# An attention of channels and a gated layer: the gate's bias through ScalarE, and transposes of v on 32-bit words

## The chip, the cores and the metric

One NeuronCore of a Trainium2 chip runs the whole program. Its engines work side by side, each through its own queue in order: TensorE (PE; its weight loads are shown as PEld), VectorE (DVE), ScalarE (ACT), GpSimd (POOL, which here issues the loads) and SyncE (SP, which issues the stores). They hand work over by semaphores. Matmul results go to PSUM, a small memory that VectorE and ScalarE read and write too; everything else is in SBUF. The metric is the device time of one execution in microseconds.

## The reference

For each of 4 batches, q, k and v are 6336 rows of 256 channels. The attention is over channels, not rows: one 256 x 256 matrix for a batch.

```python
qn = q / (norm of q over the rows + 1e-6);  kn likewise
s  = kn.T @ qn / tau                    # 256 x 256, per batch
a  = softmax(s, axis=-1)
x  = v @ a                              # 6336 x 256
H  = relu(x @ w_h);  T = sigmoid(x @ w_t + b_t)
out = T * H + (1 - T) * x
```

q, k and v are 78 MB of float32 and the output 26 MB.

## The kernel before

**Tiling.** The rows of a batch are cut into 50 slices: 48 of 128 rows and two of 96. In a load, each partition takes rows that lie next to each other, eight slices to a tile (`CH = 8`), and the DMA casts to fp16. Two slices are a *pair*; there are 25 pairs to a batch and 100 in all, numbered g = 25 b + i.

**Stage 1** (`stage1`, L354 to L356) goes over the slices of q and k and accumulates three products in the PSUM tile `sg`: k.T q, and the diagonal blocks of k.T k and q.T q, whose diagonals are the squared norms. For each half c of the channels, a slice takes three matmuls, of 256, 128 and 128 columns, each with a weight load of its own.

**The chain** (`plan_chain`) then makes the softmax on 256 x 256 (L391 to L557), transposes it, multiplies it by the two weight matrices (L590) and leaves `mr`, 256 x 768 in fp16: the columns of a, of a @ w_h and of a @ w_t. It uses VectorE, ScalarE and TensorE in turn. Its broadcast (L512) is the one matmul on fp32 numbers.

**Stage 2** runs over pairs. `transposes` (L628) turns the pair's v, four blocks of 128 x 128 fp16, into the PSUM tile `vt`; `evac_vt` (L634) copies it to SBUF on ScalarE as `vtsb`; `main_xh` (L641) multiplies it by the first 512 columns of mr, for x and x @ w_h, into `xh`. `main_t` multiplies it by the last 256 columns for the gate, into the PSUM tile `t`. A matmul with 512 columns opens t (L653): its weights `row0` are ones in one row and zero elsewhere, its columns `btb` hold the bias in that row, so that every row of t starts as the bias; the four matmuls of L656 add to it. ScalarE then makes relu into `hh` (L676) and the gate as a tanh into `uu` (L684); VectorE makes hh - x (L693), and, for two pairs at a time, the product with the gate (L703) and the result (L722), which SyncE stores.

**Order.** `Plan` is a planner that runs before the kernel is emitted. Each task has an engine, a key, a pitch and a latency in us, the tasks it depends on and the rings of buffers that it takes and gives back (`take`, `drop`). The planner plays the tasks through in time; on TensorE, ScalarE and VectorE it starts, of the tasks that are ready, the one with the lowest key, and the order that it finds becomes each engine's instruction order. Loads go out in the order of their keys. `ENDS` says at which pair stage 1 of batches 1, 2 and 3 is to end: its slices and the loads of q and k are spread evenly over the pairs before (`slot_of`). So stage 1 of the next batch runs between the pairs of the batch before it. The PSUM rings have one buffer each for `sg`, `vt` and `t`, and two for `xh`.

Of the kernel before, what the change touches and what calls it, by code (L numbers as in the profile page):

```python
# [10 lines left out]
f32 = mybir.dt.float32  # L11
f16 = mybir.dt.float16
i32 = mybir.dt.int32

P = 128
# [1 line left out]
QK_BUFS = 9  # L17
V_BUFS = 7
HEAD = 8
ENDS = [16, 41, 68]  # L20


class Ring:
# [136 lines left out]
def kernel(  # L160
# [11 lines left out]
    nc = tc.nc  # L172
    B, N, C = q.shape
# [5 lines left out]
    S = N // P // CH * CH  # L179
# [4 lines left out]
    NP = NS // 2  # L184
    assert NP % 2 == 1

    const = ctx.enter_context(tc.tile_pool(name="consts", bufs=1))
# [7 lines left out]
    plan = Plan()  # L195
# [11 lines left out]
    def new(tag, shape, dt, name):  # L207
        return pool_of.get(tag, work).tile(shape, dt, tag=tag, bufs=nbuf[tag], name=name)


    ident0 = const.tile([P, P], f32, tag="ident0")
    ident = const.tile([P, P], f16, tag="ident")
    ones = const.tile([P, P], f32, tag="ones")
    row0 = const.tile([P, P], f16, tag="row0")
    btb = const.tile([P, 2, C], f16, tag="btb")
    wht = const.tile([P, 2, 2 * C], f16, tag="wht")

    def constants():
# [39 lines left out]
    def sub(nm, b, s):  # L258

        if s < S:  # L260
            return tiles[(nm, b, s // CH)][:, s % CH, :]
        return tiles[(nm, b, NJ)][0:TR, s - S, :]

    def rows(s):
        return P if s < S else TR
# [32 lines left out]
    consts = plan.add("POOL", len(plan.tasks), 0.6, 1.5, [], constants)  # L298
# [45 lines left out]

    def stage1(b, s):

        if s == 0:
            sg_t[b] = new("sg", [P, 2, 512], f32, f"sg{b}")
        sg = sg_t[b]
        qa, ka = sub("q", b, s), sub("k", b, s)  # L350
        first, last = s == 0, s == NS - 1
        for c in range(2):
            cs = bass.ts(c, P)
            nc.tensor.matmul(sg[:, c, 0:C], ka[:, cs], qa, start=first, stop=False)  # L354
            nc.tensor.matmul(sg[:, c, C : C + P], ka[:, cs], ka[:, cs], start=False, stop=False)  # L355
            nc.tensor.matmul(  # L356
                sg[:, c, C + P : C + 2 * P], qa[:, cs], qa[:, cs], start=False, stop=last
            )
# [3 lines left out]
    mr_own = {}  # L362
# [253 lines left out]
    vt_sb = {}  # L616
    vt_ps = {}
    xh_t = {}
    og = {}
    el = {}  # L620

    def transposes(b, i):
        ps = new("vt", [P, 2, 2, P], f16, f"vtps{b}_{i}")
        nr = rows(2 * i)
        for u in range(2):
            src = sub("v", b, 2 * i + u)
            for c in range(2):
                nc.tensor.transpose(ps[:, u, c, 0:nr], src[:, bass.ts(c, P)], ident[0:nr, 0:nr])  # L628
        vt_ps[(b, i)] = ps

    def evac_vt(b, i):
        nr = rows(2 * i)
        vt_sb[(b, i)] = vt = new("vtsb", [P, 2, 2, P], f16, f"vtsb{b}_{i}")
        nc.scalar.copy(out=vt[:, :, :, 0:nr], in_=vt_ps.pop((b, i))[:, :, :, 0:nr])  # L634

    def main_xh(b, i):
        mr, vt, nr = mr_t[b], vt_sb[(b, i)], rows(2 * i)
        xh = new("xh", [P, 2, 2 * C], f32, f"xh{b}_{i}")
        for u in range(2):
            for kt in range(2):  # L640
                nc.tensor.matmul(  # L641
                    xh[0:nr, u, :],
                    vt[:, u, kt, 0:nr],
                    mr[kt][:, 0 : 2 * C],
                    start=(kt == 0),
                    stop=(kt == 1),
                )
        xh_t[(b, i)] = [xh]

    def main_t(b, i):  # L650
        mr, vt, nr = mr_t[b], vt_sb.pop((b, i)), rows(2 * i)
        tt = new("t", [P, 2, C], f32, f"t{b}_{i}")
        nc.tensor.matmul(tt[0:nr, :, :], row0[:, 0:nr], btb, start=True, stop=False)  # L653
        for u in (1, 0):
            for kt in range(2):
                nc.tensor.matmul(  # L656
                    tt[0:nr, u, :],
                    vt[:, u, kt, 0:nr],
                    mr[kt][:, 2 * C : 3 * C],
                    start=False,  # L660
                    stop=(kt == 1 and u == 0),
                )
        xh_t[(b, i)].append(tt)


    def groups_of(b):

        full = NP - 3 if b == B - 1 else NP - 1
        return [[i, i + 1] for i in range(0, full, 2)] + [[i] for i in range(full, NP)]

    def relu(b, i, grp):
        nr, o = rows(2 * i), 2 * (i - grp[0])
        if i == grp[0]:
            for nm in ("hh", "uu", "dd"):
                el[(nm, b, i)] = new(nm, [P, 4, C], f32, f"{nm}{b}_{i}")
        nc.scalar.activation(  # L676
            out=el[("hh", b, grp[0])][0:nr, o : o + 2, :],
            in_=xh_t[(b, i)][0][0:nr, :, C : 2 * C],
            func=Act.Relu,
        )  # L680

    def gate(b, i, grp):
        nr, o = rows(2 * i), 2 * (i - grp[0])
        nc.scalar.activation(  # L684
            out=el[("uu", b, grp[0])][0:nr, o : o + 2, :],
            in_=xh_t[(b, i)][1][0:nr, :, :],
            func=Act.Tanh,
            scale=-0.5,
        )
# [49 lines left out]
            )  # L739


    ready = {}

    def plan_stage1(b):
# [13 lines left out]
    last_o = {}  # L758

    def plan_stage2(b):  # L760
        tr, ev, xh, tt = {}, {}, {}, {}
        for i in range(NP):
            g = b * NP + i
            deps = loaded("v", b, 2 * i) + loaded("v", b, 2 * i + 1) + [consts]
            tr[i] = plan.add(
                "PE", g - 1.6, 0.22, 0.42, deps, lambda i=i: transposes(b, i),
                take=["vt", "vtsb"], drop=drops("v", b, 2 * i + 1),
            )
            ev[i] = plan.add(
                "ACT", g - 1.5, 0.5, 0.64, [tr[i]], lambda i=i: evac_vt(b, i),  # L770
                drop=[(tr[i], "vt")],
            )
            xh[i] = plan.add(
                "PE", g, 0.86, 1.06, [ev[i]] + ready[b], lambda i=i: main_xh(b, i), take=["xh"]
            )
            tt[i] = plan.add(
                "PE", g + 0.1, 0.64, 0.84, [xh[i]] + b_ld, lambda i=i: main_t(b, i),
                take=["t"], drop=[(tr[i], "vtsb")] + ([(mr_own[b], "mr0"), (mr_own[b], "mr1")]
                                                      if i == NP - 1 else []),
            )  # L780
        for grp in groups_of(b):
            us = []
            for i in grp:
                g = b * NP + i
                h = plan.add(
                    "ACT", g, 0.5, 0.63, [xh[i]], lambda i=i, grp=grp: relu(b, i, grp),
                    take=["hh", "uu", "dd"] if i == grp[0] else [],
                )
                h0 = h if i == grp[0] else h0
                us.append(  # L790
                    plan.add(
                        "ACT", g + 0.1, 0.5, 0.63, [tt[i], h],
                        lambda i=i, grp=grp: gate(b, i, grp), drop=[(tt[i], "t")],
                    )
                )
                us.append(
                    plan.add(
                        "DVE", g + 0.2, 0.6, 0.72, [h], lambda i=i, grp=grp: diff(b, i, grp),
                        drop=[(xh[i], "xh")],
                    )  # L800
                )
            d = 0.07 + 0.533 * len(grp)
            m = plan.add(
                "DVE", g + 1.2, d, d + 0.12, us, lambda grp=grp: product(b, grp),
                drop=[(h0, "uu")],
            )
            s = 2 * grp[0]
            j, o, n = s // CH, s % CH, 2 * len(grp)
            tag = "ot" if s >= S else "o"
            r = plan.add(  # L810
                "DVE", g + 1.9, d, d + 0.12, [m], lambda grp=grp: result(b, grp),
                take=[tag] if s >= S or o == 0 else [], drop=[(h0, "hh"), (h0, "dd")],
            )
            if s >= S:
                plan.add(
                    "SP", g + 2, 0.1, 0, [r], lambda: store(b, NJ, 0, 2), drop=[(r, "ot")],
                    size=TR * 2 * C * 4,
                )
                continue
            if o == 0:  # L820
                own = r
            split = b == B - 1 and j == NJ - 1
            if split or o + n == CH:
                lo, cnt = (o, n) if split else (0, CH)
                plan.add(
                    "SP", g + 2, 0.1, 0, [r], lambda j=j, lo=lo, cnt=cnt: store(b, j, lo, cnt),
                    drop=[(own, "o")] if o + n == CH else [], size=P * cnt * C * 4,
                )
# [45 lines left out]
```

## Time and profile before

| | |
|---|---|
| Runs | 307.14, 308.60 and 308.69 us; median 308.6 |
| Profiled execution | 307.13 us, span 305.3 us |
| TensorE busy | 274.8 us (90% of the span), granted clock 0.996 |
| VectorE busy | 204.6 us (67%) |
| ScalarE busy | 178.5 us (58%) |
| HBM | 78.4 MB read, 26.0 MB written |

The span goes from the first to the last instruction of the program; the 1.8 us between it and the execution's time lie around it. Busy time is the union of an engine's instructions. Matmuls are pipelined: the duration of one (222 ns for 128 columns, say) is longer than the step from one to the next, and where the text speaks of the step, it is from the chain of waits, which counts each piece of time once. "x" with a number is a count of instructions.

### The profile page before, as it was taken

What the parts mean: (1) busy time and instruction counts of PE and PEld (TensorE: products, weight loads), DVE (VectorE), ACT (ScalarE), POOL (GpSimd) and SP (SyncE); (2) the same over time, 40 slices, a digit from 0 to 9 for tenths busy, and PEclk for the clock granted to TensorE, in tenths of its full rate; (3) what the DMA queues carried; (4) which work ended last, traced back from release to release, by engine and by line L of the source; (5) the groups of instructions that cost most, each with busy time, mean ns of one, the idle gap of its engine ahead of it and who ended that gap; (6) DMA issues with size and microseconds to landing.
All of it is one profiled execution on the core that took longest, in us unless ns stands there. A gap on an engine that the chain in (4) does not pass through costs nothing.

```text
span 305.3 us, 6171 instructions
## 1 busy us (share of the span) xinstructions
PE 274.8 (90%) x2540; PEld 200.0 (66%) x2540; DVE 204.6 (67%) x321; ACT 178.5 (58%) x336; POOL 48.7 (16%) x96
## 2 busy tenths in 40 slices
PE   0886867999999999999999999999999789999981
PEld 0775855777777777777776777777777445666640
DVE  1000042576677978667677987676767998999995
ACT  1000043565656686666667676666666788998862
POOL 7222442221131221121212121100001000000000
PEclk9999999999999999999999999999999999999998
DMA  6999999999999999999999999999875334333334
GB/s 124 213 215 207 214 208 214 213 233 260 278 244 250 281 216 276 285 226 274 279 247 247 281 232 261 284 250 249 233 207 167 57 137 166 132 143 140 138 138 164
DMA packets 16828, 65.54 MB, mean 215 GB/s; under 512 B 1952, under 2 KB 3616, under 8 KB 13856
## 3 DMA queue, kind: packets, MB, share of 16 engines
q0 software_dynamic: 12608, 39.20, 65.3%
q1 hardware_dynamic: 4192, 25.95, 21.2%
q8 instruction: 20, 0.33, 0.4%
q14 instruction: 8, 0.07, 0.1%
HBM read 78.38 MB, written 25.95 MB: 342 GB/s over the span
## 4 chain that ended last, share of the span: by engine, by line
PE 63%; DVE 18%; DMA 9%; issue 3%; ACT 3%; POOL 1%; ACTq 0%; DVEq 0%; POOLq 0%
PE xh L641 20%; PE sg L354 11%; PE t L656 10%; PE sg L355 6%; PE sg L356 6%; DMA q<-in_q_dram 6%; DVE o L722 6%; DVE dd L693 5%; PE vtps L628 5%; PE t L653 5%; DVE dd L703 5%; DMA k<-in_k_dram 4%; PE ah L590 1%; DVE junk L391 1%; ACT hh L676 1%
## 5 line engine op out<-in xcount | busy, mean ns | idle before, releaser
L354 PE MATMUL sg<-q,k 128*128 128x256 f16 x384 | 93.0, 276 | 14.6 <-DMA k<-in_k_dram 13.9
L641 PE MATMUL xh<-mr,vtsb 128*128 128x512 f16 (+1 forms) x400 | 102.7, 379 | 2.7 <-ACT mr L601 1.6
L693 DVE TENSOR_TENSOR dd<-hh,xh 128x512 f32<-128x512 f32 (+1 forms) x100 | 68.0, 683 | 37.2 <-ACT hh L676 37.1
L676 ACT ACTIVATE hh<-xh 128x512 f32<-128x512 f32 (+1 forms) x100 | 59.6, 597 | 45.8 <-PE xh L641 24.5
L355 PE MATMUL sg<-k 128*128 128x128 f16 x384 | 85.1, 222 | 0.0
L356 PE MATMUL sg<-q 128*128 128x128 f16 x384 | 85.1, 222 | 0.0
L684 ACT ACTIVATE uu<-t 128x512 f32<-128x512 f32 (+1 forms) x100 | 60.4, 604 | 28.7 <-PE t L656 28.5
L703 DVE SCALAR_TENSOR_TENSOR dd<-uu,dd 128x1024 f32<-128x1024 f32 (+2 forms) x53 | 61.6, 1163 | 14.3 <-ACT uu L684 12.9
L656 PE MATMUL t<-mr,vtsb 128*128 128x256 f16 (+1 forms) x400 | 60.0, 273 | 0.0
L722 DVE SCALAR_TENSOR_TENSOR o<-dd,hh 128x1024 f32<-128x1024 f32 (+1 forms) x49 | 58.8, 1200 | 1.0
L634 ACT COPY vtsb<-vtps 128x512 f16<-128x512 f16 (+1 forms) x100 | 57.7, 577 | 2.3 <-PE vtps L628 2.2
L641 PEld LDWEIGHTS <-vtsb 128*128 128x128 f16 (+1 forms) x400 | 36.6, 99 | 29.0 <-issue 4.2
L354 PEld LDWEIGHTS <-k 128*128 128x128 f16 x384 | 38.0, 99 | 21.2 <-DMA k<-in_k_dram 14.6
L656 PEld LDWEIGHTS <-vtsb 128*128 128x128 f16 (+1 forms) x400 | 39.4, 99 | 17.6 <-issue 3.1
L355 PEld LDWEIGHTS <-k 128*128 128x128 f16 x384 | 38.1, 99 | 7.7 <-issue 1.1
L356 PEld LDWEIGHTS <-q 128*128 128x128 f16 x384 | 38.0, 99 | 4.8
L653 PE MATMUL t<-btb,row 128*128 128x512 f16 (+1 forms) x100 | 37.9, 379 | 2.5 <-ACT uu L684 2.5
L628 PE MATMUL vtps<-ident,v 128*128 128x128 f16 x384 | 37.1, 219 | 0.2 <-ACT vtsb L634 0.2
L628 PEld LDWEIGHTS <-v 128*128 128x128 f16 x384 | 29.3, 98 | 9.8 <-issue 0.6
L391 DVE SCALAR_TENSOR_TENSOR junk<-sg,ident 128x128 f32<-128x128 f32 x16 | 4.6, 290 | 35.2 <-PE sg L356 34.8
L254 POOL DMA_DIRECT2D v<-in_v_dram x24 | 12.8, 532 | 80.6 <-PE vtps L628 45.2
L417 ACT ACTIVATE inv<-x 128x4 f32<-128x4 f32 x1 | 0.2, 205 | 38.1 <-DVE junk L391 38.1
(61 smaller groups left out, 116.0 us busy)
## 6 DMA issues: line engine op xcount, KB each, us to landing
out_dram<-o SPq DMA_DIRECT2D x23, 1024.0 KB, 8.8
v<-in_v_dram POOLq DMA_DIRECT2D x24, 512.0 KB, 20.3
q<-in_q_dram POOLq DMA_DIRECT2D x23, 512.0 KB, 20.3
k<-in_k_dram POOLq DMA_DIRECT2D x23, 512.0 KB, 20.5
out_dram<-ot SPq DMA_DIRECT2D x4, 192.0 KB, 6.7
q<-in_q_dram POOLq DMA_DIRECT2D x2, 256.0 KB, 14.6
k<-in_k_dram POOLq DMA_DIRECT2D x2, 256.0 KB, 11.3
out_dram<-o SPq DMA_DIRECT2D x1, 512.0 KB, 2.7
```

The costliest lines, as they stand in the source:

```text
L354: nc.tensor.matmul(sg[:, c, 0:C], ka[:, cs], qa, start=first, stop=False)
L355: nc.tensor.matmul(sg[:, c, C : C + P], ka[:, cs], ka[:, cs], start=False, stop=False)
L356: nc.tensor.matmul(sg[:, c, C + P : C + 2 * P], qa[:, cs], qa[:, cs], start=False, stop=last)
L628: nc.tensor.transpose(ps[:, u, c, 0:nr], src[:, bass.ts(c, P)], ident[0:nr, 0:nr])
L634: nc.scalar.copy(out=vt[:, :, :, 0:nr], in_=vt_ps.pop((b, i))[:, :, :, 0:nr])
L641: nc.tensor.matmul(xh[0:nr, u, :], vt[:, u, kt, 0:nr], mr[kt][:, 0 : 2 * C], start=(kt == 0), stop=(kt == 1),)
L656: nc.tensor.matmul(tt[0:nr, u, :], vt[:, u, kt, 0:nr], mr[kt][:, 2 * C : 3 * C], start=False, stop=(kt == 1 and u == 0),)
L676: nc.scalar.activation(out=el[("hh", b, grp[0])][0:nr, o : o + 2, :], in_=xh_t[(b, i)][0][0:nr, :, C : 2 * C], func=Act.Relu,)
L684: nc.scalar.activation(out=el[("uu", b, grp[0])][0:nr, o : o + 2, :], in_=xh_t[(b, i)][1][0:nr, :, :], func=Act.Tanh, scale=-0.5,)
L693: nc.vector.tensor_tensor(out=el[("dd", b, grp[0])][0:nr, o : o + 2, :], in0=el[("hh", b, grp[0])][0:nr, o : o + 2, :], in1=xh_t[(b, i)][0 ...
L703: nc.vector.scalar_tensor_tensor(out=dd[0:nr, 0:n, :], in0=el[("uu", b, grp[0])][0:nr, 0:n, :], scalar=1.0, in1=dd[0:nr, 0:n, :], op0=AluO ...
L722: nc.vector.scalar_tensor_tensor(out=ot, in0=el[("dd", b, grp[0])][0:nr, 0:n, :], scalar=-0.5, in1=el[("hh", b, grp[0])][0:nr, 0:n, :], op ...
```

## The change

The gate's bias is written into `t` by ScalarE ahead of the gate's matmuls for the pairs g up to `PRESET` = 68. A new constant `bias_all` holds the bias on all partitions in fp32: one matmul at the start spreads it (`spread`), one copy on ScalarE brings it to SBUF (`spread_out`). For each of those pairs a copy on ScalarE (`bias`) takes the buffer of t and fills it, and the gate's four matmuls add to what stands there; L653 falls away. From pair 69 on, L653 is as before.

v is transposed as words of 32 bits, each holding two neighbouring fp16 channels: two transposes of 128 words in place of four of 128 fp16, against the fp32 identity. In `vt` and `vtsb` the even and odd channels of a row then lie alternately, so the weights of `main_xh` and `main_t` are read with a step of two, one half for even and one for odd channels. So that `mr` has its rows in the same order, stage 1 takes k's channels with a step of two as well, as weights (L354, L355) and as columns (L355).

The planner's numbers for these tasks change, `ENDS` goes from 16, 41, 68 to 18, 43, 69, and two edges of dependence are added (the second relu of a group after the first, a result after the one that opened its output tile).

```diff
-ENDS = [16, 41, 68]
+PRESET = 68
+ENDS = [18, 43, 69]
...
+    bias_all = const.tile([P, 2, C], f32, tag="bias_all")
...
         for c in range(2):
             cs = bass.ts(c, P)
-            nc.tensor.matmul(sg[:, c, 0:C], ka[:, cs], qa, start=first, stop=False)
-            nc.tensor.matmul(sg[:, c, C : C + P], ka[:, cs], ka[:, cs], start=False, stop=False)
+            kc = ka.rearrange("p (w two) -> p two w", two=2)[:, c, :]
+            nc.tensor.matmul(sg[:, c, 0:C], kc, qa, start=first, stop=False)
+            nc.tensor.matmul(sg[:, c, C : C + P], kc, kc, start=False, stop=False)
...
     def transposes(b, i):
-        ps = new("vt", [P, 2, 2, P], f16, f"vtps{b}_{i}")
+        ps = new("vt", [P, 2, P], f32, f"vtps{b}_{i}")
         nr = rows(2 * i)
         for u in range(2):
-            src = sub("v", b, 2 * i + u)
-            for c in range(2):
-                nc.tensor.transpose(ps[:, u, c, 0:nr], src[:, bass.ts(c, P)], ident[0:nr, 0:nr])
+            words = sub("v", b, 2 * i + u).bitcast(f32)
+            nc.tensor.transpose(ps[:, u, 0:nr], words, ident0[0:nr, 0:nr])
         vt_ps[(b, i)] = ps
 
     def evac_vt(b, i):
         nr = rows(2 * i)
-        vt_sb[(b, i)] = vt = new("vtsb", [P, 2, 2, P], f16, f"vtsb{b}_{i}")
-        nc.scalar.copy(out=vt[:, :, :, 0:nr], in_=vt_ps.pop((b, i))[:, :, :, 0:nr])
+        vt = new("vtsb", [P, 2, P], f32, f"vtsb{b}_{i}")
+        nc.scalar.copy(out=vt[:, :, 0:nr], in_=vt_ps.pop((b, i))[:, :, 0:nr])
+        vt_sb[(b, i)] = [
+            [vt[:, u, :].bitcast(f16).rearrange("p (n two) -> p two n", two=2)[:, kt, :] for kt in range(2)]
+            for u in range(2)
+        ]
...
-                    vt[:, u, kt, 0:nr],
+                    vt[u][kt][:, 0:nr],
...
+    def preset(b, i):
+        return b * NP + i <= PRESET
+
+    def bias(b, i):
+        nr = rows(2 * i)
+        tt_new[(b, i)] = tt = new("t", [P, 2, C], f32, f"t{b}_{i}")
+        nc.scalar.copy(out=tt[0:nr, :, :], in_=bias_all[0:nr, :, :])
+
     def main_t(b, i):
         mr, vt, nr = mr_t[b], vt_sb.pop((b, i)), rows(2 * i)
-        tt = new("t", [P, 2, C], f32, f"t{b}_{i}")
-        nc.tensor.matmul(tt[0:nr, :, :], row0[:, 0:nr], btb, start=True, stop=False)
+        if preset(b, i):
+            tt = tt_new.pop((b, i))
+        else:
+            tt = new("t", [P, 2, C], f32, f"t{b}_{i}")
+            nc.tensor.matmul(tt[0:nr, :, :], row0[:, 0:nr], btb, start=True, stop=False)
...
+    def spread():
+        bb = new("t", [P, 2, C], f32, "bb")
+        nc.tensor.matmul(bb, row0, btb, start=True, stop=True)
+        xh_t["bb"] = bb
+
+    def spread_out():
+        nc.scalar.copy(out=bias_all, in_=xh_t["bb"])
+
+    sp = plan.add("PE", -1, 0.22, 0.5, b_ld + [consts], spread, take=["t"])
+    b_all = plan.add("ACT", 0.5, 0.5, 0.63, [sp], spread_out, drop=[(sp, "t")])
...
             tr[i] = plan.add(
-                "PE", g - 1.6, 0.22, 0.42, deps, lambda i=i: transposes(b, i),
+                "PE", g - 1.6, 0.11, 0.33, deps, lambda i=i: transposes(b, i),
...
             ev[i] = plan.add(
-                "ACT", g - 1.5, 0.5, 0.64, [tr[i]], lambda i=i: evac_vt(b, i),
+                "ACT", g - 1.5, 0.29, 0.42, [tr[i]], lambda i=i: evac_vt(b, i),
...
+            own = []
+            if preset(b, i):
+                own = [
+                    plan.add("ACT", g - 0.05, 0.5, 0.63, [b_all], lambda i=i: bias(b, i), take=["t"])
+                ]
             tt[i] = plan.add(
-                "PE", g + 0.1, 0.64, 0.84, [xh[i]] + b_ld, lambda i=i: main_t(b, i),
+                "PE", g + 0.1, 0.43 if own else 0.64, 0.63 if own else 0.84,
+                [xh[i]] + b_ld + own, lambda i=i: main_t(b, i), take=[] if own else ["t"],
...
```

More of the change, by code (lines that the diff above doesn't have):

```diff
@@ L618 @@
     xh_t = {}
+    tt_new = {}
     og = {}
@@ L657, in main_t @@
                     tt[0:nr, u, :],
-                    vt[:, u, kt, 0:nr],
+                    vt[u][kt][:, 0:nr],
                     mr[kt][:, 2 * C : 3 * C],
@@ L661, in main_t @@
                     stop=(kt == 1 and u == 0),
+                    skip_group_check=preset(b, i),
                 )
@@ L760, in plan_stage2 @@
     def plan_stage2(b):
-        tr, ev, xh, tt = {}, {}, {}, {}
+        tr, ev, xh, tt, own_t = {}, {}, {}, {}, {}
         for i in range(NP):
@@ L775, in plan_stage2 @@
             )
+            own = []
[3 more added lines that the diff above has]
+                ]
             tt[i] = plan.add(
-                "PE", g + 0.1, 0.64, 0.84, [xh[i]] + b_ld, lambda i=i: main_t(b, i),
-                take=["t"], drop=[(tr[i], "vtsb")] + ([(mr_own[b], "mr0"), (mr_own[b], "mr1")]
+                "PE", g + 0.1, 0.43 if own else 0.64, 0.63 if own else 0.84,
+                [xh[i]] + b_ld + own, lambda i=i: main_t(b, i), take=[] if own else ["t"], drop=[(tr[i], "vtsb")] + ([(mr_own[b], "mr0"), (mr_own[b], "mr1")]
                                                       if i == NP - 1 else []),
             )
+            own_t[i] = own[0] if own else tt[i]
         for grp in groups_of(b):
@@ L785, in plan_stage2 @@
                 h = plan.add(
-                    "ACT", g, 0.5, 0.63, [xh[i]], lambda i=i, grp=grp: relu(b, i, grp),
+                    "ACT", g, 0.5, 0.63, [xh[i]] + ([h0] if i > grp[0] else []), lambda i=i, grp=grp: relu(b, i, grp),
                     take=["hh", "uu", "dd"] if i == grp[0] else [],
@@ L792, in plan_stage2 @@
                         "ACT", g + 0.1, 0.5, 0.63, [tt[i], h],
-                        lambda i=i, grp=grp: gate(b, i, grp), drop=[(tt[i], "t")],
+                        lambda i=i, grp=grp: gate(b, i, grp), drop=[(own_t[i], "t")],
                     )
@@ L810, in plan_stage2 @@
             r = plan.add(
-                "DVE", g + 1.9, d, d + 0.12, [m], lambda grp=grp: result(b, grp),
+                "DVE", g + 1.9, d, d + 0.12, [m] + ([own] if 0 < o and s < S else []), lambda grp=grp: result(b, grp),
                 take=[tag] if s >= S or o == 0 else [], drop=[(h0, "hh"), (h0, "dd")],
```

## The prediction

> **What bounds the kernel now.** I read the page's slices first, then the engines' busy time by stage, then the chain of waits.
>
> ```profile
> span 305.3 us, 6171 instructions
> ...
> PE   0886867999999999999999999999999789999981
> ...
> DMA  6999999999999999999999999999875334333334
> ...
> core 0: us, PE busy (x) PEld busy (x) DVE busy (x) ACT busy (x) POOL busy (x), PEclk, DMA share, GB/s
> 49.00:235.00 186.00, 185.18 (x1760) 137.04 (x1760) 135.00 (x197) 120.07 (x225) 30.59 (x58) 1.00 1.02 249
> 235.00:255.00 20.00, 16.25 (x115) 9.88 (x114) 19.16 (x48) 15.65 (x32) 0.00 (x0) 1.00 0.36 101
> 255.00:300.00 45.00, 42.48 (x304) 25.88 (x302) 42.52 (x50) 37.50 (x72) 0.00 (x0) 1.00 0.39 156
> ```
>
> Three regimes. Until about 40 us batch 0's q and k are loaded and TensorE waits for them. From 49 to 235 us TensorE is busy 185.18 of 186 us; VectorE has 135 and ScalarE 120. The DMA engines are full as well (share 1.02). After 235 us stage 1 is over, the DMA share falls to 0.36, and VectorE is full (19.16 of 20 us) beside TensorE.
>
> Busy matmul time is modelled, so I check in the chain that TensorE's rows stand shoulder to shoulder (start, us):
>
> ```profile
> 120.09 0.22 PE vtps L628 x4
> 120.31 0.11 PE sg L354
> 120.42 0.06 PE sg L355
> 120.48 0.06 PE sg L356
> ...
> 120.75 0.86 PE xh L641 x4
> ...
> 122.06 0.21 PE t L653
> 122.27 0.44 PE t L656 x4
> ...
> 123.38 0.86 PE xh L641 x4
> ```
>
> They do. One pair costs 0.22 (transposes) + 0.86 + 0.215 (bias) + 0.44 = 1.74 us, one slice of stage 1 is 2 x (0.11 + 0.055 + 0.055) = 0.44, and 1.74 + 2 x 0.44 = 2.62, which is 123.38 - 120.75. So a microsecond off TensorE here is a microsecond off the run, as long as the data is there and ScalarE keeps up.
>
> **The change, part by part.**
>
> *Bias matmuls.* PRESET = 68 takes the one of L653 from pairs 0 to 68, which are those that start before stage 1 ends:
>
> ```profile
> 0.00:235.80 235.80, 26.19 (x69) 6.80 (x69) 1.00 1.02 238
> ...
> 0.00:222.70 222.70, 91.95 (x380) 37.66 (x381) 1.00 1.04 242
> 222.70:234.90 12.20, 4.70 (x20) 1.94 (x20) 1.00 0.62 185
> ```
>
> The first row counts L653 (69 before 235.8 us), the other two L354 (two to a slice: slice 190 starts near 222.7, slice 200 ends near 234.9). TensorE loses 69 x 0.215 = **-14.9 us**, all of it in the full stretch. A new one at the start (`spread`, with a ScalarE copy) runs while batch 0's chain leaves TensorE idle: 0.
>
> *What takes their place on ScalarE.* Each preset pair gains a copy of 512 fp32 per partition from SBUF into PSUM. No row writes PSUM from ScalarE. The nearest copies:
>
> ```profile
> L410 ACT COPY gs<-sg 128x512 f32<-128x512 f32 x4 | 2.3, 584 | 0.1
> ...
> L634 ACT COPY vtsb<-vtps 128x512 f16<-128x512 f16 x96 | 55.8, 582 | 1.5 <-PE vtps L628 1.5
> L634 ACT COPY vtsb<-vtps 128x384 f16<-128x384 f16 x4 | 1.9, 476 | 0.8 <-PE vtps L628 0.8
> L676 ACT ACTIVATE hh<-xh 128x512 f32<-128x512 f32 x96 | 57.2, 597 | 44.1 <-PE xh L641 24.2 <-ACT vtsb L634 11.4 <-DVE o L722 4.9
> L684 ACT ACTIVATE uu<-t 128x512 f32<-128x512 f32 x96 | 58.0, 604 | 27.5 <-PE t L656 27.5
> ...
> L608 DVE CAST mr<-ah 128x512 f16<-128x512 f32 x1 | 0.7, 692 | 1.1 <-PE ah L590 1.1
> ```
>
> Bounds 0.48 (a 384-wide copy) and 0.69 (the slowest row of a 512-wide copy, on another engine); I take 0.58, from the 512-wide fp32 copy. The evacuation of the transposes shrinks to 256 words: (582 - 476) / 128 = 0.83 ns an element, so 582 - 256 x 0.83 = 0.37 us, 0.21 less. ScalarE then has 0.60 + 0.60 + 0.58 + 0.37 = 2.15 us a pair, against a TensorE period of 2.62 - 0.215 = 2.40.
>
> The wait that is added is a ring: `t` has one buffer, so gate(i-1), bias(i), matmuls t(i), gate(i) follow each other. Its handovers stand in the chain:
>
> ```profile
> 161.61 0.45 PE t L656 x4
> 162.09 0.61 ACT uu L684
> ...
> PE t L653 <- ACT uu L684: 2.5, 2, 1.3
> ```
>
> From the end of t to the gate is 0.03 us. The ring takes 0.61 + 0.58 + 0.45 and three handovers, about 1.75 us, inside 2.40. Outside gate and bias ScalarE has 0.56 us of it and the spare 0.65, 1.21 in all, in which relu and evacuation (0.97) have to fit. They do in the steady state. It doesn't while a batch's chain puts its exponentials, copies and casts on ScalarE (some 4 us by the 0.5 to 0.6 us rows above). Behind a late bias stands all of TensorE, whose queue is in order: transposes and stage 1 of the next pairs too. Two chains lie in the preset stretch; I charge 1 us each: **+2 us**, between 0 and 14.9 (the gain itself).
>
> *Transposes.* Four fp16 of 128 columns become two fp32. The only fp32 matmul here is the broadcast L512, 256 columns wide, in two passes:
>
> ```profile
> 171.19 0.49 PE cqb L512 x2
> ...
> L512 PEld LDWEIGHTS cqb<-dcat,ones 128*128 128x128 f32 x8 | 1.3, 189 | 2.9 <-DVE dcat L500 2.7
> ...
> L628 PEld LDWEIGHTS <-v 128*128 128x128 f16 x384 | 29.3, 98 | 9.8 <-issue 0.6
> ```
>
> A pass takes 0.245 us where 256 fp16 columns take 0.11, and an fp32 weight load 189 ns against 98. Three readings for a pair: one pass at the fp32 column rate is 2 x 0.11 = 0.22, as much as now, and the two longer weight loads equal the four short ones (0.38, 0.39); two passes give 0.44, +0.22 a pair; one pass at the fp16 rate gives 0.11, -0.11. I take the middle one, the nearest to both rows: **0**, with both ends kept: -0.11 x 70 = -7.7 and +0.22 x 70 = +15.4 us.
>
> [...]
>
> *Strides of two.* The weights of L354 and L355 and the columns of L355 now step over every other fp16, as do the weights of L641 and L656. No row here has a strided operand. At full speed nothing changes: 0. At half speed, a weight load that now fits under a 0.055 us matmul would take 0.11, so L354 (loaded under L356) comes 0.055 late twice a slice; L641 and L656 load under 0.11 or more. I take 0, because the elements asked for are the same number; the other end is 300 x 0.055 = +16.5 us over the 150 slices of batches 1 to 3.
>
> *ENDS.* Stage 1 of batch 3 ends by pair 69 in place of 68: one pair more before it (1.74 - 0.215 = +1.5) and one less after (-1.75). Loads of q and k move behind some of v. Is the data there? The last full k tile of batch 3:
>
> ```profile
> 175.10 0.53 POOL L254 DMA_DIRECT2D k<-in_k_dram  x1 [3.46 <-DMA v<-in_v_dram]
> ...
> k<-in_k_dram POOLq DMA_DIRECT2D x23, 512.0 KB, 20.5
> ```
>
> Issued at 175.1, with the median 20.5 us it lands at 195.6; it is used from slice 190, at 222.7. TensorE lags its data by 27 us there. Of this the change takes 14 for its lead, 2 for a v tile that now goes ahead in GpSimd's queue (0.5 MB at the 249 GB/s of the first stage) and 6 for stores that come 5 to 6 pairs earlier (1.4 MB): 5 us are left, so the lead can be cashed in.
>
> *The end.* From 255 us both engines run at a pair in 1.74 us:
>
> ```profile
> 259.14 1.22 DVE L722 SCALAR_TENSOR_TENSOR o<-dd,hh 128x1024 f32<-128x1024 f32 x1
> ...
> 260.28 0.68 DVE L693 TENSOR_TENSOR dd<-hh,xh 128x512 f32<-128x512 f32 x1
> ...
> 262.21 0.68 DVE L693 TENSOR_TENSOR dd<-hh,xh 128x512 f32<-128x512 f32 x1
> 262.81 1.22 DVE L722 SCALAR_TENSOR_TENSOR o<-dd,hh 128x1024 f32<-128x1024 f32 x1
> ...
> 259.95 1.03 PE L641 MATMUL xh<-mr,vtsb 128*128 128x512 f16 x4
> ...
> 261.69 1.03 PE L641 MATMUL xh<-mr,vtsb 128*128 128x512 f16 x4
> ```
>
> VectorE needs 1.14 each for the product and the result of two pairs (L722 to L693) and 0.60 for each difference: 3.48 for two. Less work on TensorE or ScalarE gains nothing here.
>
> **The sum**, on the profiled execution's 307.13 us (span 305.3 and 1.8 around it; the runs' median of 308.6 is 1.5 above, their lowest 307.14): 307.1 - 14.9 + 2 + 1.5 - 1.75 = **294**.
>
> **The rivals.**
>
> [...]
>
> *ScalarE's ring sets the pace.* If a relu lands between gate and bias, the ring is 1.75 + 0.60 = 2.35 us, and with the evacuation too 2.72; at a mean of 2.53 each pair loses 0.13 of its 0.215: 294 + 69 x 0.13 = 303. For it: 2.15 of 2.40 us is 90% of ScalarE. Against: L653 waited for the gate 2.5 us in all until now.
>
> *The loads set the pace.* DMA share 1.02 to 235 us and stores that come earlier: gain lost, about 306. Against: the 5 us that are left by the median landing.
>
> *Strided weights at half speed: slower.* 294 + 16.5 = 310, from batch 1's stage 1 on, decided as soon as a strided load exceeds the 0.055 us of L356 by more than 0.04 us (12 us over 300). [...]
>
> *Two-pass transposes: slower.* 294 + 15.4, and 0.22 x 25 = 5.5 at the end, where TensorE would pass VectorE: 315. For it: both rows of L512.
>
> **Chances.** My forecast 0.40 (its own range 290 to 299), fast transposes 0.20, ring 0.14, loads 0.07, strided weights 0.11, two passes 0.08. About 0.5% (1.5 us) can be told from no change. Faster: 0.40 + 0.20 + 0.14 and 0.02 of the loads = 0.76; same 0.05, the rest of the loads; slower 0.19, the last two. The range of 285 to 308 leaves out the last two, 0.19.
>
> **What would show it.** L653's successor with 31 records and the first pairs' t matmuls released by ScalarE; TensorE still full from 50 us, with a period of 2.40; stage 1 done near 222 us. The rows of sg at 0.11, 0.055, 0.055 clear the strides; 0.22, 0.11 or 0.44 for two transposes names which reading holds; copies of 0.37 and 0.58 on ScalarE. TensorE's t waiting for ScalarE for more than 5 us in total, gaps at sg for k, or a sum of sg over 0.44 a slice would make the forecast wrong.

## The result, and the profile after

The changed kernel takes 296.95 us (median; 295.76 to 297.28), the kernel before 307.87 in the same series: a ratio of 0.9638, 95% interval 0.9594 to 0.9683. The forecast was 294, its range 285 to 308. The profiled execution took 295.76 us, with a span of 294.0.

Of the kernel after: the slices of its page, then the busy time by stage (its stage 1 ends 12 us earlier than in the kernel before, and so the second and third stage begin 12 us earlier).

```profile
span 294.0 us, 5734 instructions
...
PE   0785868999999999999999899999998789999981
...
DMA  6999999999999999999999999999999334333334
```

```profile
49.00:223.00 174.00, 172.37 (x1556) 130.73 (x1555) 134.78 (x198) 139.97 (x292) 30.57 (x58) 1.00 1.06 258
223.00:243.00 20.00, 15.89 (x96) 9.15 (x94) 19.10 (x46) 13.85 (x33) 0.00 (x0) 1.00 0.53 163
243.00:288.00 45.00, 42.41 (x261) 26.39 (x259) 42.31 (x50) 33.74 (x71) 0.00 (x0) 1.00 0.39 155
```

The picture is the old one, shorter: TensorE full (172.37 of 174 us) until stage 1 is over, then VectorE. ScalarE went from 120 of 186 us to 140 of 174. The chain of waits in the full stretch:

```profile
118.31 0.86 PE xh L650 x4
...
119.62 0.44 PE t L679 x4
120.05 0.22 PE vtps L633 x2
...
120.72 0.86 PE xh L650 x4
```

Two word transposes take 0.22 us, as four of fp16 did. No bias matmul stands before t, and a pair with its two slices takes 120.72 - 118.31 = 2.41 us in place of 2.62. The groups by shape that answer the disputed prices, and the wait on the new ring:

```profile
L639 ACT COPY vtsb<-vtps 128x256 f32<-128x256 f32 x96 | 35.5, 370 | 1.3 <-PE vtps L633 1.2
...
L668 ACT COPY t<-bias_all 128x512 f32<-128x512 f32 x67 | 40.3, 602 | 0.8
...
L633 PEld LDWEIGHTS vtps<-ident,v 128*128 128x128 f32 x192 | 23.9, 141 | 8.2 <-ACT vtsb L639 1.6
```

```profile
PE t L679 <- ACT t L668: 0.7, 1, 0.7
```

The evacuation takes 0.37 us, the bias copy 0.60, an fp32 weight load for a transpose 141 ns. TensorE waited for a bias copy once, for 0.7 us, at 162 us.

Last, VectorE's work behind stage 1. The first row is the kernel before from the end of its stage 1 to its last instruction, the second the kernel after; the fourth pair of numbers is VectorE.

```profile
234.60:305.40 70.80, 59.13 (x421) 36.12 (x419) 64.26 (x100) 53.31 (x103) 0.19 (x1) 0.98 0.37 134
```

```profile
223.10:294.10 71.00, 58.21 (x354) 35.52 (x352) 64.20 (x99) 47.85 (x102) 0.00 (x0) 0.96 0.42 153
```

Both are 71 us long and hold 64.2 us of VectorE. So the whole gain lies ahead of the end of stage 1.

### The profile page after: what moved, and what is told of

Same layout as the page of the kernel before. It is cut to its first block, busy times and chain, and to the rows that moved or that the text cites. A ratio compares the mean times of both kernels' runs of the same rounds, so it can differ in the third digit from the quotient of the medians.

```text
span 294.0 us, 5734 instructions
## 1 busy us (share of the span) xinstructions
PE 262.0 (89%) x2272; PEld 193.6 (66%) x2272; DVE 204.2 (69%) x321; ACT 194.5 (66%) x406; POOL 48.7 (17%) x96
## 4 chain that ended last, share of the span: by engine, by line
PE 62%; DVE 19%; DMA 10%; issue 4%; ACT 3%; POOL 1%; ACTq 0%; DVEq 0%; POOLq 0%
PE xh L650 21%; PE sg L358 11%; PE t L679 10%; PE sg L359 6%; PE sg L360 6%; DMA q<-in_q_dram 6%; DVE o L746 5%; DVE dd L717 5%; PE vtps L633 5%; DMA k<-in_k_dram 4%; DVE dd L727 4%; PE ah L594 1%; DVE junk L395 1%; ACT hh L700 1%; ACT uu L708 1%
## 5 line engine op out<-in xcount | busy, mean ns | idle before, releaser
L360 PE MATMUL sg<-q 128*128 128x128 f16 x384 | 84.1, 219 | 0.0
L708 ACT ACTIVATE uu<-t 128x512 f32<-128x512 f32 (+1 forms) x100 | 59.8, 598 | 22.7 <-PE t L679 21.6
L679 PE MATMUL t<-mr,vtsb 128*128 128x256 f16 (+1 forms) x400 | 59.9, 272 | 0.8 <-ACT t L668 0.7
L650 PEld LDWEIGHTS <-vtsb 128*128 128x128 f16 (+1 forms) x400 | 37.9, 99 | 30.2 <-issue 4.7
L679 PEld LDWEIGHTS <-vtsb 128*128 128x128 f16 (+1 forms) x400 | 36.9, 98 | 14.3 <-issue 5.4
L668 ACT COPY t<-bias_all 128x512 f32<-128x512 f32 (+1 forms) x69 | 41.5, 602 | 0.8
L639 ACT COPY vtsb<-vtps 128x256 f32<-128x256 f32 (+1 forms) x100 | 36.8, 368 | 1.3 <-PE vtps L633 1.2
L633 PE MATMUL vtps<-ident,v 128*128 128x128 f32 x192 | 37.0, 274 | 0.0
L633 PEld LDWEIGHTS vtps<-ident,v 128*128 128x128 f32 x192 | 23.9, 141 | 8.2 <-ACT vtsb L639 1.6
```

The lines of the kernel that those rows point to most:

```text
L360: nc.tensor.matmul(sg[:, c, C + P : C + 2 * P], qa[:, cs], qa[:, cs], start=False, stop=last)
L633: nc.tensor.transpose(ps[:, u, 0:nr], words, ident0[0:nr, 0:nr])
L650: nc.tensor.matmul(xh[0:nr, u, :], vt[u][kt][:, 0:nr], mr[kt][:, 0 : 2 * C], start=(kt == 0), stop=(kt == 1),)
L668: nc.scalar.copy(out=tt[0:nr, :, :], in_=bias_all[0:nr, :, :])
L679: nc.tensor.matmul(tt[0:nr, u, :], vt[u][kt][:, 0:nr], mr[kt][:, 2 * C : 3 * C], start=False, stop=(kt == 1 and u == 0), skip_group_check= ...
L708: nc.scalar.activation(out=el[("uu", b, grp[0])][0:nr, o : o + 2, :], in_=xh_t[(b, i)][1][0:nr, :, :], func=Act.Tanh, scale=-0.5,)
```

## The experiments

Theory: the gain is the 69 bias matmuls on TensorE, paid until stage 1 ends; words and strides move nothing; behind stage 1 VectorE's remaining work sets the time. Rivals: the words help through ScalarE; the ring through t or the loads are the next bound. Each time is a median beside runs of the kernel before on the same chip.

### One part of the change at a time

The bias by ScalarE without words and strides:

```diff
-            kc = ka.rearrange("p (w two) -> p two w", two=2)[:, c, :]
+            kc = ka[:, cs]
...
-        ps = new("vt", [P, 2, P], f32, f"vtps{b}_{i}")
+        ps = new("vt", [P, 2, 2, P], f16, f"vtps{b}_{i}")
...
-        vt = new("vtsb", [P, 2, P], f32, f"vtsb{b}_{i}")
+        vt = new("vtsb", [P, 2, 2, P], f16, f"vtsb{b}_{i}")
```

> The changed kernel with the fp16 transposes, their 512-wide evacuation and unstrided operands of the kernel before; the bias by ScalarE and ENDS as changed. Theory (the gain is the 69 bias matmuls, and back-to-back ScalarE instructions overlap by 0.1 us): four instructions at a step of 0.5 us make 2.0 us of ScalarE in a period of 2.40, so nothing is lost: 296 to 298 us, TensorE's wait for the bias copy under 2 us in all. Rival (the durations count in full): 0.58 + 0.60 + 0.60 + 0.58 = 2.36 of 2.40 us leaves no room, the ring through t sets the pace and the kernel takes 301 us or more; then the words would be worth 4 us or more through ScalarE.

300.33 us, ratio 0.9741 (0.9694 to 0.9787): between the two, 3.4 us over the full change. TensorE's stage 1 ended early, at 220.7 us, but at pair 67, and preset pairs stood behind it. Before I put that on ScalarE, I took those away:

```diff
-PRESET = 68
+PRESET = 64
```

> The kernel with the bias by ScalarE alone (fp16 transposes), PRESET = 64. In that kernel stage 1 ended at pair 67 and preset pairs stood behind it, with a half clock from 229 us. Theory: that is part of its 300.3 us, as with the old ENDS: 298 to 299.3 us and no half clock there. Rival: ScalarE is too full in the whole stretch (2.36 of 2.40 us), and fewer presets only give matmuls back to TensorE: 300 to 301.5 us.

297.25 us, ratio 0.9647 (0.9616 to 0.9677); the changed kernel beside it took 297.23. The theory's 298 to 299.3 was too cautious, and a shorter stretch of half clock is left: the granted clock is 0.76 from 227 to 234 us. In this kernel's full stretch, ScalarE (fourth pair) and its four groups read:

```profile
49.00:219.00 170.00, 168.69 (x1664) 128.08 (x1664) 130.34 (x193) 144.62 (x280) 29.53 (x56) 1.00 1.06 257
```

```profile
L698 ACT ACTIVATE hh<-xh 128x512 f32<-128x512 f32 (+1 forms) x66 | 39.8, 604 | 5.7 <-PE xh L648 5.0 <-DVE o L744 0.3 <-DVE ri L542 0.3
L640 ACT COPY vtsb<-vtps 128x512 f16<-128x512 f16 (+1 forms) x67 | 39.1, 583 | 1.2 <-PE vtps L634 1.1
L706 ACT ACTIVATE uu<-t 128x512 f32<-128x512 f32 (+1 forms) x65 | 39.0, 600 | 16.2 <-PE t L677 15.4 <-PE vtps L634 0.6
L666 ACT COPY t<-bias_all 128x512 f32<-128x512 f32 (+1 forms) x64 | 38.8, 606 | 0.6
```

Durations of 0.60 + 0.58 + 0.60 + 0.61 would be 2.4 us a pair, all of the period. But these four groups add up to 156.7 us, more than the 144.6 us in which ScalarE is busy at all: instructions that follow each other overlap, so durations overstate ScalarE. It is busy 85% of the stretch, and the gate still waits 15.4 us for its matmuls.

So the bias by ScalarE, with the new ENDS and with PRESET in its place, brings the whole gain; words and strides add nothing that can be told. It gets there by another split than the changed kernel: stage 1 ends 3.7 us earlier, and more of VectorE's work stands behind it, 68.26 us in place of 64.20:

```profile
219.40:295.20 75.80, 63.56 (x444) 38.60 (x441) 68.26 (x104) 56.53 (x110) 1.04 (x2) 0.96 0.45 159
```

What the new ENDS alone would do to the kernel before stays open, and so does the changed kernel with PRESET = 64.

The other half alone (the changed kernel without presets and with the old ENDS):

```diff
-PRESET = 68
-ENDS = [18, 43, 69]
+PRESET = -1
+ENDS = [16, 41, 68]
```

> The changed kernel with no pair preset (every bias by the matmul) and ENDS as before: the transposes on words, the strides and the 0.37 us evacuation alone. Theory: two word transposes at 0.109 us a step are as long as four at 0.056, the strided weights add about 0.003 us a load, ScalarE isn't the bound: 307.5 to 309.5 us, no difference that can be told. Rival: the lighter evacuation speeds the waits of TensorE and of the end, 303 to 306 us.

307.83 us, ratio 0.9973 (0.9955 to 0.9991): 0.8 us faster, inside the theory's range and far from the rival's 303 to 306. And the strides alone, in the kernel before:

```diff
+            kc = ka.rearrange("p (w two) -> p two w", two=2)[:, c, :]
-            nc.tensor.matmul(sg[:, c, 0:C], ka[:, cs], qa, start=first, stop=False)
+            nc.tensor.matmul(sg[:, c, 0:C], kc, qa, start=first, stop=False)
...
-            src = sub("v", b, 2 * i + u)
+            src = sub("v", b, 2 * i + u).rearrange("p (w two) -> p two w", two=2)
```

> The kernel before with k's channels and the weights of v's transposes read with a step of two, still four fp16 transposes to a pair, nothing else. Theory: a strided weight load takes some 3 ns more than the 55 ns that hide it, twice a slice over 150 slices and four times a pair: 0.8 to 2 us, so 308.5 to 310 us against 307.9. Rival: no cost at all, under 0.3 us; or a full second read for each, 16 us and more.

Ratio 0.9999 (0.9979 to 1.0018): no cost that can be measured, less than I had expected, and the 16 us of a second read are excluded. The weights of `main_xh` and `main_t` have no step of two in this run; in the run with words alone they have.

### Where stage 1 ends, and where the presets end

```diff
-ENDS = [18, 43, 69]
+ENDS = [16, 41, 68]
```

> The changed kernel with ENDS 16, 41, 68 of before. Theory (TensorE's work sets the time until stage 1 ends, VectorE's work that is left sets the rest): stage 1 ends a pair earlier, at about 221.5 us, and the rest is 0.6 to 1.8 us longer, 296 to 298 us, no difference that can be told from 297. Rival (q and k loads are the next bound, since they land 3 to 9 us ahead of their use in the changed kernel): stage 1 that comes earlier waits for its data, 299 us or more, with TensorE idle on k.

300.57 us, ratio 0.9726 (0.9701 to 0.975). The time is the rival's, its reason isn't: the longest wait of TensorE behind the first batch is not for k. In the planner's order stage 1 ended not one pair earlier but four (at 219.7 us, pair 66). TensorE's instructions behind that end:

```profile
221.92 0.60 PE L679 MATMUL t<-mr,vtsb 128*128 128x256 f16 x4
...
224.23 0.60 PE L679 MATMUL t<-mr,vtsb 128*128 128x256 f16 x4 [1.50 <-ACT t L668]
...
226.55 0.71 PE L679 MATMUL t<-mr,vtsb 128*128 128x256 f16 x4 [1.51 <-ACT t L668]
```

With no slices of stage 1 to put between, a preset pair takes 2.31 us, and TensorE idles 1.5 us in each. This is the ring with one more ScalarE instruction on it between gate and bias: in the first of the two pairs the copy of sg that belongs to batch 3's chain (0.48 us), in the second a relu. The chain of waits of the second:

```profile
224.93 0.60 ACT uu L708
225.52 0.49 ACT hh L700
226.01 0.50 ACT t L668
```

Then TensorE's granted clock (the number before the DMA share) falls:

```profile
219.70:226.90 7.20, 4.20 (x32) 2.83 (x31) 6.58 (x28) 5.29 (x12) 1.04 (x2) 1.00 0.84 232
226.90:233.70 6.80, 6.22 (x21) 3.29 (x19) 6.08 (x12) 4.20 (x11) 0.00 (x0) 0.50 0.70 180
233.70:244.90 11.20, 10.64 (x69) 6.60 (x67) 9.64 (x12) 9.12 (x19) 0.00 (x0) 1.00 0.32 131
```

To part the presets from the place of the end:

```diff
-PRESET = 68
-ENDS = [18, 43, 69]
+PRESET = 64
+ENDS = [16, 41, 68]
```

> The changed kernel with ENDS 16, 41, 68 and PRESET = 64, so that the bias copies stop where stage 1 ends there. Theory: what the old ENDS cost was mostly that four preset pairs stood behind the end of stage 1, where the ring holds TensorE back and its clock halves for 6.8 us; without them 297 to 298.5 us, no half clock near 230 us. Rival: stage 1 that ends earlier leaves 7 us more of VectorE's work behind it, and that is the cost whatever PRESET is: 299.5 to 301 us.

298.81 us, ratio 0.9703 (0.9677 to 0.973). The half clock near 230 us is gone: from the end of stage 1 on, the mean granted clock is 0.96, as in the changed kernel, against 0.93 with PRESET = 68. What that gained can't be told from these runs: it is 0.7 us by the ratios (0.9726 and 0.9703, whose intervals overlap) and 1.8 us by the medians. In the kernel with the bias alone, the same step from PRESET = 68 to 64 brought 3.1 us, clear of both intervals. Against the changed kernel (297.23 us, ratio 0.964) 1.6 us remain, so the rival holds at least in part. What remains is VectorE's: stage 1 ends 3.7 us earlier (219.4 against 223.1), and 70.97 us of VectorE lie behind it, not 64.20:

```profile
219.40:297.30 77.90, 65.06 (x397) 39.70 (x395) 70.97 (x107) 52.93 (x114) 1.04 (x2) 0.96 0.44 157
```

In the other direction:

```diff
-PRESET = 68
-ENDS = [18, 43, 69]
+PRESET = 70
+ENDS = [18, 43, 71]
```

> The changed kernel with ENDS 18, 43, 71 and PRESET = 70. Theory (TensorE until stage 1 ends, VectorE's work that is left behind it): two pairs more before at 1.52 us, two fewer after at 1.74 to 1.87, and fewer pairs left to fill the chain of batch 3: 0 to -0.7 us against the changed kernel beside it, no difference that can be told. Rival: the chain stands bare and TensorE idles long enough for the half clock, 2 us or more slower.

300.36 us, ratio 0.9734 (0.9704 to 0.9764): 3.1 us slower than the changed kernel beside it, so the rival. Stage 1 ended at pair 72. VectorE had 2 us less left, but the rest stayed as long. The first row is that rest, the other two lie in batch 3's chain:

```profile
227.60:298.70 71.10, 56.32 (x339) 34.77 (x337) 62.01 (x97) 47.98 (x101) 0.00 (x0) 0.95 0.35 137
232.00:238.00 6.00, 2.55 (x12) 1.19 (x11) 5.76 (x17) 3.41 (x9) 0.00 (x0) 0.95 0.13 53
238.00:244.00 6.00, 4.46 (x24) 2.67 (x23) 4.46 (x5) 4.22 (x9) 0.00 (x0) 0.77 0.30 123
```

Too few pairs were left to fill batch 3's chain: TensorE is busy 2.55 of 6 us, its granted clock then falls to 0.77 in the mean, and VectorE, which ought to be full here, is busy 4.46 of 6 us. Presets for all pairs:

```diff
-PRESET = 68
+PRESET = 99
```

> The changed kernel with PRESET = 99: ScalarE writes the bias of every pair. Theory: without slices of stage 1 between the pairs the ring through t (gate, bias, matmuls) is the pace, 2.3 us a pair by the 221.92, 224.23 and 226.55 us starts in the kernel with the old ENDS, against 1.74: 30 pairs lose 0.3 to 0.55 us each, 305 to 314 us. Rival: TensorE has 0.215 us a pair less to do, VectorE sets the end as before, 296 to 298 us.

312.11 us, ratio 1.0143 (1.0104 to 1.0182), slower than before the change. Near the end, the chain of waits of two pairs reads:

```profile
262.74 1.89 PE xh L650 x8
264.62 0.45 PE t L679 x4
...
265.16 0.60 ACT uu L708
265.75 0.26 ACT vtsb L639
266.02 0.49 ACT t L668
266.51 0.53 ACT hh L700
...
267.07 0.70 DVE dd L717
...
267.81 0.81 PE xh L650 x3
```

Two pairs take 267.81 - 262.74 = 5.07 us, 2.53 each, where VectorE's work makes it 1.83 in the changed kernel (its results for two pairs lie 3.66 us apart). The theory's time holds, its ring is too short: the relu waits behind the bias copy on ScalarE, the difference waits for the relu, and the next xh for the difference. So the pace is one long cycle through both t and xh.

### What bounds next

A kernel with one transpose a pair and half the evacuation (v of each pair's second slice is left out, the first stands in for it):

```diff
-        for u in range(2):
+        for u in range(1):
...
-        nc.scalar.copy(out=vt[:, :, 0:nr], in_=vt_ps.pop((b, i))[:, :, 0:nr])
+        nc.scalar.copy(out=vt[:, 0, 0:nr], in_=vt_ps.pop((b, i))[:, 0, 0:nr])
```

> The changed kernel with one word transpose a pair in place of two and an evacuation of half the width: v of the second slice of each pair is left out, the first slice's stands in for it. It asks what bounds next. Theory: TensorE is still the bound until stage 1 ends, 0.109 us a pair over 70 pairs is 7.6 us, less what the loads (3 to 9 us ahead of their use now) take back: 291 to 293 us. Rival: the loads are as good as the bound already, 295 us or more, with TensorE waiting for k or v.

294.89 us, ratio 0.9585 (0.955 to 0.9621): some 2 us of the 7.6, and the interval still overlaps the changed kernel's. Neither theory holds. Of its waits from 48 to 221 us:

```profile
PEld L679 <- issue: 4.0, 6, 1.2
PE t L679 <- ACT t L668: 3.0, 5, 1.0
...
PE xh L650 <- DVE dd L717: 1.6, 3, 1.0
```

TensorE waits for t and for xh, and for no load of k or v there; for t it waits 3.0 us in place of the changed kernel's 0.7. As far as these waits name it, the next bound is the handover through the PSUM rings; whether a different order of the same work would avoid it stays open, since the planner made a new order for this kernel.

VectorE's end, tried with GpSimd:

```diff
+        if on_pool(b, grp):     # b == 3, two pairs, grp[0] % 6 == 2
+            nc.gpsimd.tensor_scalar(out=dd, in0=dd, scalar1=-0.5, ...)
+            nc.gpsimd.tensor_tensor(out=ot, in0=dd, in1=hh, op=AluOp.add)
```

> The changed kernel with four of batch 3's eleven double results on GpSimd, as a product with -0.5 and a sum, in place of VectorE's one instruction. Theory: VectorE's work that is left after stage 1 sets the end; 4 x 1.14 = 4.6 us go off it, 292 to 294 us if GpSimd takes under 5 us for the two. Rival: GpSimd's two instructions are slower than that, or hold hh and dd so long that relu waits for its buffer: 297 us or more.

314.18 us, ratio 1.02 (1.0164 to 1.0235): the rival, and more.

```profile
L748 POOL TENSOR_SCALAR dd<-dd 128x1024 f32<-128x1024 f32 x4 | 11.1, 2772 | 60.6 <-DVE dd L727 60.6
L751 POOL TENSOR_TENSOR o<-dd,hh 128x1024 f32<-128x1024 f32 x4 | 10.9, 2732 | 0.3
```

```profile
254.31 1.22 DVE L727 SCALAR_TENSOR_TENSOR dd<-uu,dd 128x1024 f32<-128x1024 f32 x1 [0.87 <-ACT uu L708]
255.57 3.25 DVE L755 SCALAR_TENSOR_TENSOR o<-dd,hh 128x1024 f32<-128x1024 f32 x1
```

GpSimd needs 5.5 us for what VectorE does in 1.2, and the result of VectorE's own that stands here took 3.25 us, where such a result takes 1.22 in the changed kernel. The relu waited 8.2 us in all for GpSimd to be done with its buffer. Which of the two cost more isn't worked out.

### The clock in the first chain

> The changed kernel once more, beside the others of this call: 296 to 297.5 us, in two groups some 1.4 us apart.

297.23 us, ratio 0.964 (0.9605 to 0.9676). Two executions took 295.70 and 295.94 us at a mean granted clock of 0.993 and 0.992; three took 297.14 to 297.43 at 0.982 to 0.988, and one 298.75 at 0.983.

```diff
+        for n in range(6):   # after the last slice of batch 0
+            f = plan.add("PE", -40 + n, 0.45, 0.66, [x, consts], lambda n=n: fill(n), take=["xh"])
+        for m in range(8):   # in fill
+            nc.tensor.matmul(ps[:, 0, 0:P], row0, ident, start=True, stop=True)
```

> The changed kernel with 48 matmuls of 128 columns, whose results nobody reads, after the last slice of stage 1 of batch 0, where TensorE waits 2.6 us for VectorE. Theory: the executions of one kernel lie in two groups because the granted clock falls to one half near 41 us in some of them, after that idle stretch, and batch 0's chain and first pairs then start 1.5 to 2 us later; with the stretch filled none does: median 295.5 to 296 us, one group. Rival: the half clock is not due to that stretch, or the matmuls themselves delay the chain's: 296.5 us or more, two groups as before.

298.58 us, ratio 0.9687 (0.9658 to 0.9716): slower, and it settles nothing. The added tasks moved the planner's order: stage 1 ended at pair 68 with 68.14 us of VectorE behind it, the cost already seen. Its profiled execution has no half clock near 41 us, but one execution doesn't show a rule.

No kernel beat the changed one by more than the intervals.

## Why the prediction was right, point by point

*The bound.* Right: a period of 2.41 us against the forecast 2.40, and TensorE full until stage 1's end.

*The bias matmuls, -14.9 us.* Right. With the new ENDS and its presets ended in time, the bias alone took 297.25 us beside 297.23, so it needs no help from words or strides.

*The wait on ScalarE, +2 us.* Right in size, but partly by luck. Stage 1's last slice moved from 234.6 to 223.1 us, by 11.5; -14.9 + 1.5 for the pair that was added leave 1.9 for all waits. What I had charged, 1 us for a late bias copy in each of two chains, came once, with 0.7 us, in batch 2's chain at 162 us. The rest lies in other waits that I had not charged, such as 0.29 us for a difference at 203 us. The ring's price of 1.75 us was its bare sum; where slices of stage 1 no longer cover it, a pair takes 2.31 us with one more instruction on it, near the rival's 2.35, and 2.53 by the longer cycle with presets for all pairs. I had named the chains as the danger; the larger danger is the preset pairs behind the end of stage 1.

*The transposes, 0.* Right by the middle reading: 0.22 us a pair before and after. A word transpose steps at 0.109 us for 128 columns, half the 0.22 of the chain's row; a pass of L512 took 0.245 for 256 columns, which would be 0.12. The chance of 0.20 for fast transposes stood on the reading of one pass at the fp16 rate, -0.11 a pair. No run shows that rate: two word transposes took 0.22 us, not 0.11.

*The strides, 0.* Right, by the experiment on them alone: the +16.5 us of the slower rival didn't come.

*ENDS.* The +1.5 us is nearly right: 70 pairs have their xh ahead of stage 1's end, not 69, but 68 have their t there, before and after (272 matmuls of L656 and of L679). The **-1.75 us for one pair less behind it failed**: the rest took 71.0 us, as before 70.8. I had counted pairs by their xh. In the new order t comes later behind xh, so the products and results of that pair were still to come. VectorE's groups of products and results behind stage 1 count as many of both kinds as before, two rows of the kernel before and two of the kernel after, and its work is 64.20 against 64.26 us:

```profile
L703 DVE SCALAR_TENSOR_TENSOR dd<-uu,dd 128x1024 f32<-128x1024 f32 (+2 forms) x19 | 21.1, 1111 | 2.0 <-ACT uu L684 0.7
L722 DVE SCALAR_TENSOR_TENSOR o<-dd,hh 128x1024 f32<-128x1024 f32 (+1 forms) x17 | 19.7, 1156 | 0.1
```

```profile
L727 DVE SCALAR_TENSOR_TENSOR dd<-uu,dd 128x1024 f32<-128x1024 f32 (+2 forms) x19 | 21.1, 1110 | 2.1 <-ACT uu L708 1.0
L746 DVE SCALAR_TENSOR_TENSOR o<-dd,hh 128x1024 f32<-128x1024 f32 (+1 forms) x17 | 19.7, 1156 | 0.0
```

This term is the 1.7 us between the forecast and the profiled execution (295.76); the other 1.2 us to the median lie in the profiled execution, as the forecast had said. I had also misread VectorE's pace there: the results at 259.14 and 262.81 us are 3.67 us apart, so a pair takes VectorE 1.83 us, not TensorE's 1.74.

*The loads.* Right: no wait for k behind batch 0.

## What to carry to other kernels

Moving work from the full engine to a half-empty one paid nearly in full where other work covered the new handover. End it where that cover ends: behind it, it costs, and for all pairs it cost more than it had given. Count what is left for the last engine in that engine's own instructions, not in units of the loop. And test the parts of a change one by one: here one of them, with the order that suits it, brought all the gain that can be told.

## What the runs showed of the hardware

In these traces the granted TensorE clock falls to one half for 3.4 or 6.8 us behind stretches in which TensorE idles part of the time. With the old ENDS this is the row above from 226.9 us, behind two idle stretches of 1.5 us within 5. It also happens in some executions near 41 us, where the first chain holds TensorE for 2.6 us, for 3.4 us in the kernel before with strides alone:

```profile
42.70:46.10 3.40, 3.40 (x28) 2.93 (x25) 1.14 (x5) 0.98 (x4) 1.39 (x3) 0.50 1.06 213
```

The idle stretch doesn't always bring it. In the kernel with the bias alone (PRESET = 68) the clock there is 0.51, and the first pair starts at 51.88 us; in the changed kernel, with the same 2.6 us idle, it is 1.00, and the pair starts at 48.82:

```profile
41.10:48.00 6.90, 6.25 (x37) 4.89 (x38) 2.26 (x9) 3.60 (x8) 3.59 (x7) 0.51 1.07 214
```

```profile
41.10:48.00 6.90, 6.00 (x62) 4.72 (x63) 2.44 (x9) 3.69 (x9) 3.30 (x7) 1.00 1.07 215
```
